# Stores of an output tile as two DMAs, permuted reads on ScalarE, one weight in fp32 on SyncE, and a new order, in a fused attention and token-mixing kernel

## Chip, cores and metric

One core of a Trainium2 chip. The metric is the device time of one execution in microseconds. A profile is one execution, taken by the hardware profiler; its span runs from the first to the last instruction.

## The reference

Attention within chunks of 64 tokens (8 batches, 8 heads, 576 tokens, 64 channels a head), then a mixing block on the joined heads (512 channels):

```python
attn = softmax(q_c @ k_c^T / sqrt(64))        # per chunk of 64
x = (attn @ v_c)  -> (B, S, H * D)            # B=8, S=576, H*D=512
theta = x @ w_theta
zr, zi = x * cos(theta), x * sin(theta)
y = w_tok_r @ zr + w_tok_i @ zi               # over the 576 tokens
u = x + y
out = u + maximum(u @ w_ch, 0)                # float32
```

## The kernel before

The batches are taken in four pairs (0 to 3). The tokens of a pair are 9 tiles of 128 rows: four of each batch, and a middle tile (j = 4, group M) with the last 64 tokens of both. For the attention they form five groups: A and B (first batch), C and D (second), of two tiles each, and M of one.

Every step is written out by hand: ORDER (lines 18 to 60) is a list of names such as `T.0A.1`, a kind, a pair, a group or tile, and sometimes a PSUM slot. The loop at lines 530 to 533 issues them in that order, each engine takes its own instructions in that order, and an in-order engine that waits holds up all behind it. The kinds:

- `q`, `k`, `v` (lines 145 to 182): loads on POOL's DMA queue, which convert fp32 to fp16. q and k of a group share a buffer of the pool `nat` (line 111), which has eight; v has a slot for each tile of two pairs.
- `lt`, `lc`, `lw` (lines 184 to 192): loads of the weights, on POOL too; `lw.00` and `lw.01` are w_tok_r and w_tok_i, 576 KB and 72 KB each in fp16.
- `TW`, `twd`, `twa` (lines 196 to 226): transposes of the token weights on PE, and their copies out of PSUM on DVE and ACT.
- `T`, `tq`, `tk` (lines 230 to 264): transposes of q and k of a group on PE; q is copied by DVE, k by ACT (M's k by DVE). The loads put tokens 2p and 2p+1 on partition p, so the halves come out of the transpose apart; ACT's copy of k puts them together again by writing with a step of two.
- `S`, `e` (lines 266 to 301): scores on PE, exponential on ACT, which writes with a step of two as well.
- `V0`, `V1`, `v0`, `v1` (lines 303 to 336): attention times v for four heads each on PE; DVE divides by the sum of the row (reciprocal at line 328).
- `X`, `x`, `H`, `g`, `z` (lines 338 to 413): transpose of x, its copy on ACT, theta on PE, cosine and sine on ACT, products zr and zi on DVE. For the middle tile two halves change partitions by DMAs on SyncE (lines 410, 411, from `zmid`).
- `Y`, `y`, `U`, `u`, `W`, `w` (lines 417 to 492): for each of the 36 tiles the mixing over tokens on PE (nine accumulating matmuls), plus x on DVE, a transpose, its copy (ACT for even tiles, DVE for odd), the last matmul, relu and sum on DVE into `o` (one of four buffers of `outp`, line 114), and the store to HBM, one DMA on SyncE (line 492). `Y.00` needs zr and zi of groups A, B and M and the whole of wT, thus all three `TW`.

PSUM has three slots of two banks (wide) and two of one bank (thin); Y, U and W use the thin ones. The store of a tile is a DMA whose DRAM side has three dimensions, r (2), t (64) and d (512), as lines 489 to 491 write it: rows 0 to 63 and 64 to 127 of the tile are tokens 128 apart.

Of the kernel before, what the change touches and what calls it, by code (L numbers as in the profile page):

```python
# [18 lines left out]
q.0A new.10 q.0B v.0B init.00 k.0A q.0C q.0M k.0B new.00 v.0A k.0M T.0A.0 tk.0A lt.00
tq.0A S.0A.1 e.0A v.0M T.0B.2 tk.0B V1.0A.0 lw.00 tq.0B v1.0A V0.0A.1 v0.0A S.0B.2 k.0C  # L20
T.0M.0 lw.01 X.0A.1 tq.0M e.0B tk.0M q.1B S.0M.2 x.0A e.0M V1.0B.0 H.0A.1 V0.0M.2 v0.0M
g.0A v1.0B V1.0M.2 V0.0B.0 v1.0M X.0M.2 x.0M v0.0B X.0B.0 q.0D v.0C q.1M TW.00.1 x.0B
H.0M.2 z.0A twd.00 H.0B.0 g.0M k.0D z.0M g.0B T.0C.2 lc.00 twa.00 tq.0C TW.01.0 z.0B
TW.02.1 v.0D twd.01 tk.0C twa.02 S.0C.2 twd.02 twa.01 Y.00.0 Y.01.1 e.0C V1.0C.0 v.1M
y.00 V0.0C.1 q.1A T.0D.2 y.01 k.1M v0.0C U.01.0 tk.0D v1.0C Y.02.1 u.01 tq.0D U.00.0
u.00 y.02 S.0D.1 X.0C.0 e.0D q.1C U.02.1 q.2M Y.03.0 V0.0D.2 u.02 V1.0D.1 v1.0D v0.0D
q.2A x.0C H.0C.0 X.0D.1 T.1M.2 y.03 k.1A W.01.1 tk.1M k.1B q.3A x.0D w.01 W.00.0 tq.1M
U.03.1 H.0D.1 v.1A k.1C g.0C S.1M.2 w.00 u.03 k.2M W.02.0 z.0C w.02 g.0D T.1A.0 z.0D
tk.1A W.03.1 w.03 e.1M T.1B.1 Y.04.0 q.1D V0.1M.2 tq.1A tk.1B tq.1B S.1A.0 V1.1M.1 e.1A
v.2M v1.1M y.04 v0.1M Y.05.1 U.04.0 v.1B u.04 v.1C X.1M.1 V0.1A.0 V1.1A.2 q.3B v0.1A  # L30
W.04.0 v1.1A x.1M S.1B.1 X.1A.0 x.1A y.05 w.04 H.1M.2 U.05.1 u.05 H.1A.0 g.1M g.1A
Y.07.0 y.07 z.1A e.1B q.2B Y.06.1 T.1C.2 v.2B y.06 V0.1B.0 V1.1B.1 U.06.0 tk.1C v.2A
tq.1C W.05.1 q.3C v1.1B S.1C.2 u.06 e.1C k.1D T.2M.1 v0.1B X.1B.0 tq.2M W.06.0 tk.2M
V1.1C.2 x.1B V0.1C.1 w.05 q.3M U.07.1 k.2B v1.1C v0.1C w.06 v.3M u.07 k.3A v.2D H.1B.0
k.3C X.1C.2 T.1D.1 Y.08.0 z.1M x.1C W.07.1 y.08 tq.1D U.08.0 v.1D q.2D H.1C.2 g.1B w.07
z.1B u.08 W.08.1 S.2M.0 tk.1D S.1D.1 e.1D Y.10.0 e.2M w.08 g.1C y.10 k.2A Y.11.1 V0.1D.1
y.11 V1.1D.0 v1.1D Y.12.0 v0.1D X.1D.0 T.2B.2 y.12 T.2A.1 x.1D v.3A U.11.1 U.10.0 tk.2B
H.1D.0 z.1C tk.2A new.20 u.10 u.11 W.11.1 tq.2B tq.2A w.11 Y.13.0 k.3B k.2D g.1D q.2C
U.12.1 S.2B.2 z.1D y.13 u.12 v.3D V1.2M.1 e.2B v1.2M S.2A.0 Y.16.1 y.16 k.2C T.2C.1
tk.2C V0.2M.2 W.12.0 v0.2M w.12 W.10.1 tq.2C e.2A U.13.0 u.13 T.2D.2 X.2M.0 V1.2B.1  # L40
tq.2D w.10 Y.14.0 tk.2D V0.2B.2 x.2M v1.2B V0.2A.0 V1.2A.1 y.14 Y.15.1 U.14.0 v0.2A y.15
v1.2A H.2M.0 u.14 v0.2B Y.17.1 U.16.0 g.2M y.17 X.2B.1 u.16 X.2A.2 S.2C.0 W.13.1 v.3C
W.16.0 w.13 z.2M x.2A U.17.1 u.17 w.16 x.2B H.2A.2 g.2A H.2B.1 z.2A W.17.1 g.2B v.2C
v.3B w.17 Y.18.0 W.14.1 e.2C z.2B T.3A.2 tk.3A k.3M y.18 S.2D.1 V1.2C.0 Y.21.0 w.14
new.30 v1.2C tq.3A U.18.1 e.2D V0.2C.0 S.3A.2 u.18 V1.2D.1 y.21 U.15.0 v1.2D Y.22.1
T.3M.1 v0.2C u.15 e.3A X.2C.2 V0.2D.0 tq.3M Y.20.0 y.22 v0.2D y.20 W.18.1 tk.3M w.18
V0.3A.0 x.2C V1.3A.2 X.2D.1 U.22.0 v0.3A u.22 x.2D q.3D W.15.1 U.20.0 H.2C.0 w.15 u.20
W.20.1 v1.3A w.20 g.2C U.21.0 u.21 H.2D.1 Y.23.1 g.2D T.3B.2 z.2C S.3M.0 T.3C.1 e.3M
y.23 z.2D U.23.0 tk.3C u.23 W.21.1 k.3D tq.3C tq.3B Y.25.0 tk.3B V1.3M.0 w.21 v1.3M
T.3D.1 y.25 tq.3D S.3B.2 V0.3M.0 W.22.1 W.23.0 e.3B V1.3B.2 v0.3M tk.3D X.3A.0 V0.3B.1  # L50
w.22 Y.24.1 x.3A v1.3B v0.3B X.3M.2 S.3D.0 w.23 x.3M X.3B.1 y.24 U.25.0 H.3M.2 e.3D
U.24.1 u.24 u.25 Y.26.0 H.3A.0 y.26 U.26.1 g.3M u.26 Y.27.0 x.3B g.3A W.24.1 z.3M w.24
y.27 H.3B.2 U.27.1 W.25.0 g.3B S.3C.1 z.3A V1.3D.0 u.27 w.25 e.3C Y.28.1 W.27.0 V1.3C.2
z.3B v1.3D y.28 V0.3C.0 V0.3D.1 w.27 v0.3D W.26.1 v0.3C Y.30.0 v1.3C X.3D.1 X.3C.0 w.26
x.3C y.30 Y.31.1 U.30.0 x.3D y.31 u.30 H.3C.2 U.28.1 u.28 U.31.0 H.3D.0 u.31 g.3C W.28.1
W.31.0 g.3D w.28 W.30.1 w.31 z.3C w.30 Y.33.0 z.3D Y.32.1 y.33 y.32 Y.34.0 U.32.1 y.34
U.33.0 u.32 W.32.1 u.33 Y.35.0 w.32 U.34.1 y.35 U.35.0 u.34 W.33.1 u.35 W.34.0 w.33
Y.36.1 w.34 W.35.0 y.36 w.35 Y.37.1 y.37 U.36.0 U.37.1 u.36 u.37 W.36.0 Y.38.1 w.36
W.37.0 y.38 w.37 U.38.1 u.38 W.38.0 w.38
# [500 lines left out]
```

## Time and profile before

| | us |
|---|---|
| runs, median of 3 (lowest to highest) | 301.07 (300.09 to 301.48) |
| profiled execution | 300.1 |
| its span | 298.3 |
| PE matmul busy | 197.9 (66%) |
| ACT busy | 133.1 (45%) |
| DVE busy | 126.4 (42%) |
| POOL busy | 77.5 (26%) |
| granted TensorE clock, mean | 0.876 |

Busy times are of one execution. Matmuls are pipelined and their ends are modelled, so the step from one group's start to that of the next says more of PE's pace than the length of a matmul. SP is SyncE; its instructions are DMA issues and count as no busy time. A wait is put down to what came last.

### The profile page before, as it was taken

Reading aid. Unit: us, or ns where it says so; the run is one execution under the profiler, and the core shown is the slowest. Engines: PE = TensorE matmul, PEld = TensorE weight load, DVE = VectorE, ACT = ScalarE, POOL = GpSimd, SP = SyncE. Lnnn points to the kernel's source line nnn. Section 1 sums busy time; section 2 is a strip of 40 time slices with the busy share of each in tenths; the row PEclk is TensorE's granted clock in tenths of the full one; section 3 lists DMA queues with packets and bytes.
Section 4 is the critical chain, followed back from the end, with each engine's and each line's share of the span. In section 5 each row is a group of like instructions: output and inputs, shape, how many; then the busy total and the mean of one; then the engine's idle time right before and its main releaser. Section 6 shows DMA issues by size and latency. Waiting matters only on the chain.

```text
span 298.3 us, 8370 instructions
## 1 busy us (share of the span) xinstructions
PE 197.9 (66%) x3834; PEld 102.9 (34%) x3834; DVE 126.4 (42%) x248; ACT 133.1 (45%) x137; POOL 77.5 (26%) x100
## 2 busy tenths in 40 slices
PE   0347859698975006969049999998999968762000
PEld 0233425244442002445025545555545424330000
DVE  0044616276476000556016687768486444240000
ACT  1255672387785100858132787586883701000000
POOL 8965759518030017632260000000000000000000
PEclk9999768999999555999758999999999979997555
DMA  9999999999945349996898121111121111111111
GB/s 87 169 193 193 181 170 164 166 82 123 125 63 79 64 71 77 168 159 80 86 67 94 53 63 56 54 53 55 53 66 55 51 51 51 53 51 52 51 51 40
DMA packets 86859, 27.03 MB, mean 91 GB/s; under 512 B 79528, under 2 KB 82216, under 8 KB 86824
## 3 DMA queue, kind: packets, MB, share of 16 engines
q0 software_dynamic: 81504, 16.54, 64.2%
q1 hardware_dynamic: 5320, 9.96, 9.4%
...
q14 instruction: 5, 0.04, 0.0%
...
## 4 chain that ended last, share of the span: by engine, by line
DMA 44%; PE 28%; ACT 9%; POOL 4%; issue 4%; DVE 3%; DVEq 0%; ACTq 0%; POOLq 0%
DMA qk<-in_k_dram 27%; DMA out_dram<-o 17%; PE ps_y L435 10%; PE ps_theta L374 7%; PE ps_uw L471 4%; POOL v L179 2%; ACT kT L259 2%; ACT eT L296 2%; ACT cos L390 2%; POOL qk L158 2%; ACT sin L394 2%; PE ps_uT L453 1%; PE ps_qkT L241 1%; PE ps_x L316 1%; DVE x L329 1%
## 5 line engine op out<-in xcount | busy, mean ns | idle before, releaser
L435 PE MATMUL ps_y<-zr,wT 128*128 128x512 f16 (+1 forms) x180 | 45.2, 404 | 3.9 <-DVE o L480 2.8
L435 PE MATMUL ps_y<-zi,wT 128*128 128x512 f16 (+1 forms) x180 | 46.9, 395 | 0.0
L435 PEld LDWEIGHTS <-wT 128*128 128x128 f16 (+1 forms) x360 | 32.1, 104 | 42.8 <-issue 11.2
L444 DVE TENSOR_TENSOR u<-ps_y,x 128x512 f16<-128x512 f32 x36 | 24.8, 688 | 52.1 <-PE ps_y L435 51.9
L241 PE MATMUL ps_qkT<-id,qk 64*64 64x64 f16 x1152 | 16.2, 207 | 44.8 <-DMA qk<-in_k_dram 27.9
L471 PE MATMUL ps_uw<-wch,uT 128*128 128x512 f16 x144 | 38.5, 400 | 5.9 <-DVE o L480 5.6
L465 ACT COPY uT<-ps_uT 128x512 f16<-128x512 f16 x20 | 11.8, 588 | 65.8 <-PE ps_uT L453 65.8
L480 DVE SCALAR_TENSOR_TENSOR o<-ps_uw,u 128x512 f32<-128x512 f32 x36 | 24.8, 688 | 32.7 <-DMA out_dram<-o 20.2
L374 PE MATMUL ps_theta<-wtheta,xT 128*128 128x512 f16 x144 | 37.2, 405 | 0.2 <-ACT xT L361 0.2
L259 ACT COPY kT<-ps_qkT 128x1024 f16<-128x1024 f16 x16 | 20.8, 1302 | 32.6 <-PE ps_qkT L241 27.8
L179 POOL DMA_DIRECT2D v<-in_v_dram x32 | 28.3, 894 | 27.0 <-DMA qk<-in_q_dram 9.2
L241 PEld LDWEIGHTS <-qk 64*64 64x64 f16 x1152 | 13.5, 118 | 49.4 <-DMA qk<-in_k_dram 28.4
L361 ACT COPY xT<-ps_xT 128x1024 f16<-128x1024 f16 (+1 forms) x20 | 18.3, 927 | 19.3 <-PE ps_xT L349 19.3
L329 DVE TENSOR_TENSOR x<-ps_x,recip 128x512 f16<-128x512 f32 (+1 forms) x40 | 25.5, 638 | 1.4
L390 ACT ACTIVATE cos<-ps_theta,pihalf 128x1024 f16<-128x1024 f32 (+1 forms) x20 | 20.6, 1030 | 9.0 <-PE ps_theta L374 8.9
L296 ACT ACTIVATE eT<-ps_sT 128x1024 f16<-128x1024 f32 x16 | 21.0, 1310 | 6.6 <-PE ps_sT L283 6.5
L257 DVE COPY qT<-ps_qkT 128x1024 f16<-128x1024 f16 (+1 forms) x20 | 12.6, 633 | 22.0 <-ACT kT L259 19.0
L471 PEld LDWEIGHTS <-uT 128*128 128x128 f16 x144 | 13.5, 101 | 21.5 <-issue 8.2
L374 PEld LDWEIGHTS <-xT 128*128 128x128 f16 x144 | 13.9, 103 | 16.0 <-issue 3.6
L328 DVE RECIPROCAL recip<-ps_x 128x8 f32<-128x8 f32 (+1 forms) x40 | 7.8, 195 | 26.0 <-PE ps_x L316 26.0
L394 ACT ACTIVATE sin<-ps_theta 128x1024 f16<-128x1024 f32 (+1 forms) x20 | 18.7, 934 | 0.0
L158 POOL DMA_DIRECT2D qk<-in_q_dram x16 | 14.5, 908 | 13.6 <-PE ps_qkT L241 8.1
...
## 6 DMA issues: line engine op xcount, KB each, us to landing
out_dram<-o SPq DMA_DIRECT2D x36, 256.0 KB
qk<-in_q_dram POOLq DMA_DIRECT2D x16, 256.0 KB, 7.0
...
qk<-in_k_dram POOLq DMA_DIRECT2D x16, 256.0 KB, 9.4
...
qk<-in_q_dram POOLq DMA_DIRECT2D x8, 64.0 KB, 6.8
qk<-in_k_dram POOLq DMA_DIRECT2D x8, 64.0 KB, 6.9
```

The costliest lines, as they stand in the source:

```text
L179: nc.gpsimd.dma_start(v16[:, slot + r, :, 0:D], v[2 * p + bb, :, t0 : t0 + P, :].rearrange("h s d -> s h d"),)
L241: nc.tensor.transpose(psv[half[h], r, e, w, s, :], t[half[r], w, 2 * e + h, s, :], id16[half[r], half[r]],)
L259: nc.scalar.copy(out=t.rearrange("p x c t -> p x (c t)").rearrange("p x (i s) -> p x s i", s=2), in_=ps,)
L296: nc.scalar.activation(out=eT.rearrange("p h r e (i s) -> p (h r e) s i", s=2), in_=ps.rearrange("p (x s i) -> p x s i", s=2, i=CH // 2), ...
L329: nc.vector.tensor_tensor(out=st[p]["x"][:, j0 : j0 + n, f * NE * D : (f + 1) * NE * D].rearrange("p c (h d) -> p c h d", h=NE), in0=psv[: ...
L374: nc.tensor.matmul(ps[:, j * DM : j * DM + DM], xT[:, j * NDB + db, :], wtheta16[:, db, :], start=(db == 0), stop=(db == NDB - 1),)
L390: nc.scalar.activation(out=cos[:, 0:n].rearrange("p a e -> p (a e)"), in_=pin, func=AF.Sin, bias=pihalf, scale=1.0,)
L394: nc.scalar.activation(out=sin[:, 0:n].rearrange("p a e -> p (a e)"), in_=pin, func=AF.Sin)
L435: nc.tensor.matmul(ps[rows], wT[:, kt, cols], z[:, jz, :], start=(i == 0), stop=(i == 2 * KT),)
L444: nc.vector.tensor_tensor(out=u, in0=st[p].pop(("ps_y", j)), in1=st[p]["x"][:, j], op=ALU.add)
L471: nc.tensor.matmul(ps, uT[:, db * P : db * P + P], wch16[:, db, :], start=(db == 0), stop=(db == NDB - 1),)
L480: nc.vector.scalar_tensor_tensor(out=o, in0=st[p].pop(("ps_uw", j)), scalar=0.0, in1=u, op0=ALU.max, op1=ALU.add)
```

## The change

Four things. The store of a tile is two DMAs, one for each half of 64 rows. The exponential and the copy of k write in order and read PSUM with the step instead. The first token weight is loaded as fp32 by SyncE into `wraw` (which takes a buffer of the tag `zi16`) and `wend`, and a new step `cw` casts it to fp16 on ACT. And ORDER is new throughout: it begins with the token weight and group M, puts `TW.00` first on PE, all of pair 0's loads but `v.0D` ahead of `lw.01`, and moves steps everywhere; of the steps only `cw.00` is new. Its beginning:

```
lw.00 q.0M init.00 cw.00 q.0B q.0A TW.00.0 v.0M k.0M q.0C k.0A new.00 T.0M.1 new.10
tq.0M k.0B tk.0M v.0A twd.00 S.0M.2 k.0C T.0A.1 twa.00 lt.00 e.0M V0.0M.0 q.0D T.0B.2
v.0B tq.0A tk.0A S.0A.1 tk.0B tq.0B V1.0M.2 v0.0M v.0C e.0A S.0B.0 V1.0A.1 v1.0M k.0D
v1.0A T.0C.2 V0.0A.1 e.0B tq.0C lw.01 tk.0C X.0M.0 q.1A S.0C.2 v0.0A q.1B x.0M X.0A.0
e.0C q.1M v.0D x.0A H.0M.1 H.0A.2 V1.0B.0 g.0M k.1A v1.0B g.0A V0.0B.1 v0.0B V0.0C.0
v0.0C k.1B V1.0C.1 k.1M v1.0C X.0B.2 T.0D.0 x.0B z.0A q.1C tq.0D tk.0D X.0C.1 x.0C z.0M
H.0B.2 q.2M S.0D.0 lc.00 g.0B v.1M TW.01.1 v.1A twd.01 q.1D TW.02.2 twa.01 twa.02 e.0D
H.0C.1 g.0C q.2B z.0B twd.02 Y.00.0 y.00 Y.02.1 U.00.0 V1.0D.2 T.1A.0 v1.0D u.00 tq.1A
```

The part around the loads of pair 2 and the end:

```
x.1C w.04 e.2M tk.2B u.07 H.1C.2 tq.2B W.07.0 z.1D W.05.1 w.07 q.3D Y.11.0 v.2M w.05
U.10.1 new.20 V1.2M.0 g.1C u.10 S.2A.1 V0.2M.2 y.11 W.08.0 v.3C Y.12.1 e.2A z.1C k.2D
...
U.36.1 u.36 U.34.0 u.34 W.36.1 W.34.0 w.36 w.34 Y.35.1 y.35 U.37.0 U.35.1 u.37 u.35
W.37.0 Y.38.1 w.37 W.35.0 y.38 U.38.1 u.38 W.38.1 w.35 w.38
```

The code:

```diff
+    wraw = pairp.tile([P, KT, S], FP32, name="wraw", tag="zi16")
+    wend = glob.tile([CH, S], FP32, name="wend")
...
     def load_tok(ri):
         ap = (moe_w_tok_r, moe_w_tok_i)[ri]
-        nc.gpsimd.dma_start(
-            wnat[:, 0:KT, ri, :], ap[0 : KT * P, :].rearrange("(a p) s -> p a s", p=P)
-        )
-        nc.gpsimd.dma_start(wnat[0:CH, KT, ri, :], ap[KT * P : S, :])
+        if ri == 0:
+            eng, most, end = nc.sync, wraw, wend
+        else:
+            eng, most, end = nc.gpsimd, wnat[:, 0:KT, 1], wnat[0:CH, KT, 1]
+        eng.dma_start(most, ap[0 : KT * P, :].rearrange("(a p) s -> p a s", p=P))
+        eng.dma_start(end, ap[KT * P : S, :])
+
+    def cast_tok():
+        nc.scalar.copy(out=wnat[:, 0:KT, 0], in_=wraw)
+        nc.scalar.copy(out=wnat[0:CH, KT, 0], in_=wend)
...
             nc.scalar.copy(
-                out=t.rearrange("p x c t -> p x (c t)").rearrange(
-                    "p x (i s) -> p x s i", s=2
-                ),
-                in_=ps,
+                out=t.rearrange("p x c t -> p x (c t)"),
+                in_=ps.rearrange("p x s i -> p x i s"),
             )
...
         nc.scalar.activation(
-            out=eT.rearrange("p h r e (i s) -> p (h r e) s i", s=2),
-            in_=ps.rearrange("p (x s i) -> p x s i", s=2, i=CH // 2),
+            out=eT.rearrange("p h r e c -> p (h r e) c"),
+            in_=ps.rearrange("p (x s i) -> p x i s", s=2, i=CH // 2),
...
         if j == MID:
-            to = out[2 * p : 2 * p + 2, KT * P : S, :]
+            to = [out[2 * p + b, KT * P : S, :] for b in range(2)]
         else:
             bb = int(j > MID)
             jl = j - bb * (MID + 1)
-            s0 = (jl // 2) * GT
-            to = out[2 * p + bb, s0 : s0 + GT, :].rearrange(
-                "(r c t) d -> c r t d", r=2, t=CH
-            )[jl % 2]
-        nc.sync.dma_start(to, o)
+            s0 = (jl // 2) * GT + (jl % 2) * CH
+            to = [out[2 * p + bb, s0 + r * P : s0 + r * P + CH, :] for r in range(2)]
+        for r in range(2):
+            nc.sync.dma_start(to[r], o[half[r]])
```

## Rows read from the trace of the kernel before

**Rows 1.** Page, totals: busy us (share of the span), count, by engine.

```profile
PE 197.9 (66%) x3834; PEld 102.9 (34%) x3834; DVE 126.4 (42%) x248; ACT 133.1 (45%) x137; POOL 77.5 (26%) x100
```

**Rows 2.** Windows by stage: stretch, length, busy by engine, PE clock, DMA share, GB/s.

```profile
0.00:60.00 60.00, 34.67 (x958) 19.37 (x962) 20.33 (x47) 26.37 (x27) 44.55 (x61) 0.91 1.76 165
60.00:155.00 95.00, 57.33 (x1285) 30.25 (x1272) 37.85 (x75) 47.09 (x47) 31.25 (x38) 0.84 0.92 96
155.00:240.00 85.00, 82.36 (x1498) 43.24 (x1496) 55.73 (x108) 57.27 (x60) 1.74 (x2) 0.97 0.25 60
240.00:277.50 37.50, 23.51 (x119) 10.05 (x118) 12.48 (x20) 2.35 (x4) 0.00 (x0) 0.88 0.13 52
277.50:298.30 20.80, 0.00 (x0) 0.00 (x0) 0.00 (x0) 0.00 (x0) 0.00 (x0) 0.50 0.12 47
```

**Rows 3.** Timeline of DVE, last stage: start, us, instruction, idle before and its releaser.

```profile
271.64 0.69 DVE L480 SCALAR_TENSOR_TENSOR o<-ps_uw,u 128x512 f32<-128x512 f32 x1 [3.83 <-DMA out_dram<-o]
276.77 0.69 DVE L480 SCALAR_TENSOR_TENSOR o<-ps_uw,u 128x512 f32<-128x512 f32 x1 [4.44 <-DMA out_dram<-o]
```

**Rows 4.** Chain that ended last, in order of time: start, us, what.

```profile
72.29 42.13 DMA qk<-in_k_dram
...
242.83 33.82 DMA out_dram<-o x2
```

**Rows 5.** Page, DMA issues; timeline of SyncE's queue at the first stores.

```profile
out_dram<-o SPq DMA_DIRECT2D x36, 256.0 KB
...
62.77 18.06 SPq L492 DMA_DIRECT2D out_dram<-o  x5
```

**Rows 6.** Timeline of POOL, and one row of PE, before the second stage's hole ends.

```profile
100.84 0.68 POOL L172 DMA_DIRECT2D v<-in_v_dram  x1 [6.10 <-DMA v<-in_v_dram]
107.56 0.88 POOL L158 DMA_DIRECT2D qk<-in_k_dram  x1 [6.04 <-DMA v<-in_v_dram]
...
114.46 0.64 PE L241 MATMUL ps_qkT<-id,qk 64*64 64x64 f16 x32 [20.81 <-DMA qk<-in_k_dram]
```

**Rows 7.** Timeline of SyncE's queue at 171 us; window just behind it.

```profile
171.07 0.52 SPq L410 DMA_DIRECT2D zr<-zmid  x1
...
173.00:174.00 1.00, 1.00 (x7) 0.46 (x5) 0.51 (x2) 1.00 (x2) 0.00 (x0) 1.00 0.60 97
```

**Rows 8.** Timeline of PE in the dense stretch.

```profile
190.19 0.39 PE L453 MATMUL ps_uT<-id,u 128*128 128x128 f16 x4
190.42 1.89 PE L374 MATMUL ps_theta<-wtheta,xT 128*128 128x512 f16 x8
192.15 1.03 PE L471 MATMUL ps_uw<-wch,uT 128*128 128x512 f16 x4
...
196.99 0.71 PE L241 MATMUL ps_qkT<-id,qk 64*64 64x64 f16 x64
197.52 0.32 PE L283 MATMUL ps_sT<-qT,kT 64*64 64x64 f16 x16
```

**Rows 9.** Timeline of PE at the first y tile.

```profile
41.60 2.31 PE L435 MATMUL ps_y<-zr,wT 128*128 128x512 f16 x5 [1.14 <-DVE wT L223]
```

**Rows 10.** Groups of ACT by shape (busy, mean ns), then DVE's timeline at 28 us.

```profile
L296 ACT ACTIVATE eT<-ps_sT 128x1024 f16<-128x1024 f32 x16 | 21.0, 1310 | 6.6 <-PE ps_sT L283 6.5
L259 ACT COPY kT<-ps_qkT 128x1024 f16<-128x1024 f16 x16 | 20.8, 1302 | 32.6 <-PE ps_qkT L241 27.8 <-DVE qT L257 4.8
...
L394 ACT ACTIVATE sin<-ps_theta 128x1024 f16<-128x1024 f32 x16 | 16.3, 1021 | 0.0
...
27.75 0.17 DVE L328 RECIPROCAL recip<-ps_x 128x4 f32<-128x4 f32 x1
...
28.30 0.20 DVE L328 RECIPROCAL recip<-ps_x 128x8 f32<-128x8 f32 x1
```

**Rows 11.** Page, DMA issues: KB each, median us from issue to landing.

```profile
v<-in_v_dram POOLq DMA_DIRECT2D x8, 64.0 KB, 8.1
```

**Rows 12.** Timeline of PE in the last stage.

```profile
248.17 0.38 PE L453 MATMUL ps_uT<-id,u 128*128 128x128 f16 x4 [0.46 <-DVE u L444]
```

More of the change, by code (lines that the diff above doesn't have):

```diff
@@ L18 @@
 ORDER = """
[L19 to L59, printed above, removed]
+lw.00 q.0M init.00 cw.00 q.0B q.0A TW.00.0 v.0M k.0M q.0C k.0A new.00 T.0M.1 new.10
+tq.0M k.0B tk.0M v.0A twd.00 S.0M.2 k.0C T.0A.1 twa.00 lt.00 e.0M V0.0M.0 q.0D T.0B.2
@@ new lines @@
+V0.0D.1 tk.1A Y.01.0 v.1B v0.0D X.0D.2 T.1M.0 x.0D k.1D k.2B y.02 T.1B.1 y.01 tq.1M
+U.02.1 U.01.0 k.1C k.2M z.0C tk.1B v.1D H.0D.2 u.02 tk.1M u.01 S.1A.0 W.01.1 w.01 g.0D
+e.1A tq.1B W.02.0 Y.03.1 S.1B.2 V0.1A.1 S.1M.0 w.02 z.0D v0.1A e.1B q.2A e.1M Y.04.0
+V1.1M.1 V0.1M.2 y.03 q.3A V1.1A.0 y.04 Y.06.1 v1.1A v1.1M v0.1M T.1D.0 y.06 tq.1D
+V0.1B.1 v0.1B X.1A.2 tk.1D W.00.0 U.03.1 u.03 x.1A X.1M.0 x.1M q.2D T.1C.1 k.2A tk.1C
+w.00 S.1D.2 T.2M.0 U.06.1 u.06 tq.1C W.03.0 H.1M.1 e.1D tk.2M g.1M q.2C tq.2M v.1C
@@ new lines @@
+V1.1B.0 V1.1D.2 w.03 v1.1D Y.05.1 W.06.0 V0.1D.2 v1.1B X.1B.0 x.1B y.05 H.1A.1 z.1M
+v0.1D H.1B.0 Y.07.1 w.06 U.05.0 g.1A X.1D.2 S.1C.1 g.1B y.07 T.2A.0 U.04.1 u.05 z.1B
+q.3B q.3C x.1D v.2B Y.08.0 v.2A H.1D.2 e.1C u.04 V0.1C.1 z.1A tk.2A tq.2A y.08 k.2C
+V1.1C.0 U.08.1 g.1D Y.10.0 v1.1C v0.1C q.3M u.08 S.2M.0 T.2B.1 X.1C.2 y.10 W.04.0 U.07.1
+x.1C w.04 e.2M tk.2B u.07 H.1C.2 tq.2B W.07.0 z.1D W.05.1 w.07 q.3D Y.11.0 v.2M w.05
+U.10.1 new.20 V1.2M.0 g.1C u.10 S.2A.1 V0.2M.2 y.11 W.08.0 v.3C Y.12.1 e.2A z.1C k.2D
@@ new lines @@
+v0.2M w.08 v1.2M T.2C.2 S.2B.1 e.2B V1.2A.0 v1.2A v.2D Y.15.0 v.2C tk.2C V0.2A.0 tq.2C
+y.12 y.15 T.2D.1 v.3A tq.2D v0.2A V1.2B.2 v1.2B Y.14.1 V0.2B.0 tk.2D X.2M.1 y.14 X.2A.2
+U.15.0 x.2M Y.16.1 S.2D.1 x.2A v0.2B X.2B.0 k.3B y.16 S.2C.2 e.2C U.11.1 u.15 W.10.0
+u.11 Y.18.1 w.10 x.2B e.2D y.18 H.2M.2 W.11.0 w.11 U.12.1 H.2A.0 g.2M z.2M V0.2D.1
+V1.2C.2 U.18.0 u.12 W.15.1 u.18 w.15 W.12.0 v.3M w.12 v1.2C g.2A k.3C Y.17.1 V1.2D.0
+k.3A v0.2D y.17 v1.2D T.3A.2 V0.2C.1 k.3M U.16.0 W.18.1 w.18 H.2B.0 u.16 tk.3A v0.2C
@@ new lines @@
+Y.13.0 g.2B U.17.1 tq.3A X.2C.1 y.13 u.17 v.3D T.3M.2 X.2D.0 x.2C U.14.0 W.16.1 u.14
+tq.3M x.2D z.2A U.13.0 u.13 w.16 tk.3M H.2C.1 H.2D.0 g.2C W.13.0 W.14.1 T.3B.2 S.3M.1
+g.2D z.2B w.13 S.3A.0 w.14 tq.3B tk.3B e.3M Y.20.0 Y.21.1 new.30 z.2C k.3D y.20 W.17.0
+e.3A z.2D T.3D.2 V1.3A.1 w.17 tq.3D tk.3D v1.3A v.3B V1.3M.0 Y.24.0 T.3C.2 S.3B.1 v1.3M
+tk.3C y.21 V0.3A.0 y.24 U.20.1 u.20 tq.3C Y.23.0 v0.3A X.3A.2 e.3B V0.3M.0 y.23 S.3C.1
+U.21.1 e.3C W.20.0 u.21 Y.22.1 w.20 v0.3M x.3A y.22 U.24.0 H.3A.1 U.23.1 u.24 u.23
@@ new lines @@
+W.21.0 g.3A Y.28.1 V0.3C.2 V1.3B.0 w.21 v0.3C V0.3B.1 y.28 Y.27.0 W.23.1 v0.3B V1.3C.2
+v1.3B y.27 S.3D.1 w.23 X.3M.0 x.3M e.3D v1.3C Y.25.0 y.25 U.27.1 u.27 H.3M.0 W.24.0 w.24
+V1.3D.2 g.3M V0.3D.1 v1.3D W.27.1 v0.3D Y.26.0 w.27 z.3M U.22.1 y.26 X.3C.2 u.22 X.3D.0
+X.3B.1 W.22.1 w.22 U.28.0 x.3B x.3D u.28 H.3B.1 U.25.1 z.3A u.25 W.28.0 W.25.1 g.3B
+H.3D.0 x.3C w.28 U.26.0 z.3B u.26 w.25 H.3C.1 W.26.1 g.3D g.3C w.26 Y.32.0 Y.30.1 z.3C
+y.32 Y.31.0 y.30 Y.33.1 y.31 z.3D y.33 U.30.0 u.30 U.31.1 U.33.0 u.31 u.33 U.32.1 u.32
@@ L60 @@
+W.30.0 w.30 W.31.1 w.31 W.32.0 Y.37.1 w.32 y.37 Y.36.0 W.33.1 y.36 Y.34.0 w.33 y.34
+U.36.1 u.36 U.34.0 u.34 W.36.1 W.34.0 w.36 w.34 Y.35.1 y.35 U.37.0 U.35.1 u.37 u.35
+W.37.0 Y.38.1 w.37 W.35.0 y.38 U.38.1 u.38 W.38.1 w.35 w.38
 """.split()
@@ L140, in pair @@
         for name in ("x", "zr", "zi"):
-            st[p][name] = pairp.tile([P, NT, DM], FP16, name=name + "16")
+            st[p][name] = pairp.tile([P, NT, DM], FP16, name=name + "16", tag=name + "16")
     def load_qk(p, g, which):
@@ L502 @@
         "lw": lambda p, i: load_tok(i),
+        "cw": lambda p, i: cast_tok(),
         "init": lambda p, g: setup(),
```

## The prediction

> **What bounds the kernel now.** I read the totals first, then busy time by stage, then the chain and the waits inside each stage. The totals [rows 1] name no engine: PE, the busiest, is busy for 197.9 us of 298.3. The stages [rows 2] tell more. From 155 to 240 us PE is busy 82.36 of 85 us; this stretch is bound by PE. Before it, from 60 to 155, PE works 57.33 of 95 us, and after it, from 240 to 277.5, only 23.51 of 37.5. In the last 20.8 us no engine computes at all, yet the DMA column stays at 0.12 to 0.13 and 47 to 52 GB/s. That share is the key: 2 of 16 DMA engines working without pause is 0.125.
>
> The end first. The output tile's operation on DVE waits for an output buffer, and its starts stand 5.13 us apart (271.64, 276.77), each released by a store [rows 3]; five such starts in a row keep this step. 256 KB in 5.13 us is 51 GB/s, the rate of the column. So a store runs on two engines, which fits line 489: its outermost dimension, r, has two entries. The chain agrees: its last long piece is 33.82 us of stores [rows 4]. Four buffers times 5.13 us are the 20.5 us that follow the last compute. All 36 stores [rows 5] take 36 x 5.13 = 184.7 us of a queue that first gets work at 62.77.
>
> Then the middle. One k load issued at 72.29 lands 42.13 us later [rows 4], and PE, whose next transposes need it, stands still for 20.81 us [rows 6]. On POOL the following loads wait for earlier ones for about 6 us each [rows 6], again close to the cadence of a store. My reading: every load needs a part on the two engines where stores are queued, and gets one turn for each store. Both the tail and the hole in the middle are thus the same fault.
>
> **The change, part by part.** *Stores.* Each store becomes two DMAs of 64 rows by 2 KB with the 64 rows outermost. Does such a form spread? The trace has one near relative: the zmid copies on the same SyncE queue, also 64 rows outermost. Where only stores run the share is 0.13 [rows 2]; after two zmid issues at 171 us it reaches 0.60 [rows 7], which is 7.5 engines above the stores' two. So yes, for more than two; I take all 16, which makes a store 5.13 x 2/16 = 0.64 us. SyncE pays a second issue, 0.52 us [rows 7]: 36 x 0.52 = 19 us on a queue with hundreds to spare; behind them stand only the zmid copies, one or two issues late, about 1 us. The output buffers then come free long before they are asked for; the 20.5 us tail and the 5 us steps go, and so does the cause of the 6 us loads. What is late next is PE.
>
> The Trainium skill, "DMA: Bandwidth & Descriptors", section "Rules for kernel authors", speaks against this part: do not split a transfer into its two partition halves, since both halves spray over all 16 engines and serialize. By it the split would gain nothing. The row of 0.13 does not show its premise, since the unsplit store here is not on all 16.
>
> *PE's work.* It does not change: 648 matmuls 512 wide (144 theta, 360 y, 144 w), 3042 of 64 and 144 of 128 (u transposes). In the dense stretch, 8 wide ones take 1.73 us from start to the next group's start, 64 small ones 0.53, four u transposes 0.23 [rows 8]. So 648 x 0.216 + 3042 x 0.0083 + 144 x 0.0575 = 140.0 + 25.2 + 8.3 = 173.5 us at the full clock. The dense stretch had PE busy 0.97 of the time at a granted clock of 0.97 [rows 2]; if both losses counted fully its pace would be 0.94, if they overlap 0.97. I take 0.955.
>
> *Head.* In before, Y.00 starts at 41.60 [rows 9], behind the last wT copy. In the new order more stands in front of it: all of group C's attention and its theta, and the S of D. Counted through ORDER, PE has done 12.8 us of its 173.5 by then. Loads up to lw.01 are 5.8 MB as the DMA counts them (written bytes; the fp32 weight counts 1.33), at 165 GB/s [rows 2] 35 us; before it was 4.3 MB, 26 us, and compute was the later of the two. TW.01, TW.02, their copies and H.0C follow, some 6 us. So Y.00 again at about 42; between 39 and 48, because the fp32 load shares the engines with the first q and k loads.
>
> *First token weight.* POOL loses two issues of some 0.9 and 0.5 us and ACT gains two casts: 2304 and 576 elements wide, at 1.0 ns each (sin: 1021 ns for 1024 [rows 10]) 2.3 + 0.6 = 2.9 us. ACT has nothing else until k.0M has landed; on ACT only twa.00 and e.0M are queued behind, on PE T.0M is queued behind TW.00. A late landing therefore costs the head directly; it is in the 39 to 48. wraw takes a zi16 buffer that pair 1 wants only much later.
>
> *Permuted reads.* 32 ACT operations take 1310 and 1302 ns where sin of the same size takes 1021 [rows 10]. If a stride on the reading side is free, each saves 0.29 us, 9 us of ACT; if it costs as much as on the writing side, nothing. The only strided PSUM read in the trace is DVE's reciprocal: 4 elements 0.17, 8 elements 0.20 us [rows 10], so at most 0.03/4 = 7.5 ns an element, or 7.7 us for 1024. That is the far end. I take 1.1 us, near sin, since that row has the same engine, source and size and the reciprocal is another engine's operation; with ACT at 57 of 85 us in the dense stretch [rows 2], the gain hides behind PE. I count nothing for it.
>
> The Trainium skill, "SBUF — State Buffer", section "Door 1: The DMA port swizzle", says that PSUM is organized in 8-byte lines and that non-contiguous access to it slows matmuls significantly. Whether ACT's reads suffer too no row here shows; were it so, the sum would move towards the ACT rival below.
>
> *Order and buffers.* With the loads fast, what gates them is the eight qk buffers: the n-th group's load waits for the transpose of the group eight before. I followed that for every load of both orders and counted the PE work between release and use. In the new order nearly all have over 13 us. One is short: v.2M stands on POOL behind q.3D, which waits for T.2B, and V1.2M comes 7.0 us of PE work later, 7.3 at this pace. POOL needs 0.9 for q.3D and 1.4 for two v issues [rows 6], and a 64 KB v load 8.1 us to land [rows 11]: 10.4. So PE waits about 3 us; 0 to 5. In before T.2C had a similar slack, 7.9.
>
> **The sum.** Y.00 at 42; then (173.5 - 12.8)/0.955 = 168.3, which gives 210.3; v.2M 3, 213.3. At the end only y, u, w of the last tiles are left, on two PSUM slots, and gaps of 0.46 us for u appear [rows 12]: eight tiles, 4 us, 217.3. After the last Y, y and u lie open, some 1.5; then relu_add 0.69, two issues 1.0, landing 2.5 (between 0.64 of transfer plus about 1, which before's end needs beyond its cadence, and 8.1): 5.7, so 223.0. Before's profiled run took 300.1 us for a span of 298.3, 1.8 outside; so 224.8, and I say 225. Its 300.1 stands 1.0 below the median of the runs, 301.07.
>
> **The rivals.** (a) *The loads stay late.* If the 6 us turns come from something other than the stores, only the end is cured: 298.3 less 20.5, plus 3 for a new landing, less 12 of the steps between 240 and 277.5 (37.5 less 23.51 of PE work [rows 2], with 2 left over), plus 1.8, about 271. For it: the rows name only loads as what POOL waits for [rows 6]. Against it: the turns are as long as a store and a load, and before the first store the rate is 165 GB/s [rows 2]. (b) *The split does not spread.* Two halves of 2.56 us on the same two engines: cadence 5.13, time as before, 300. This is what the Trainium skill's rule on halves, above, would give. If each half ran on one engine, a tile would take 10.3 us and the end would come at 62.8 + 36 x 10.3, about 430. Against both: the 0.60 [rows 7]. (c) *ACT becomes the bound, slower.* Place: e and k copies, with PE waiting for each. ACT has 133.1 - 41.8 + 2.9 = 94.2 us of other work. With some 27 us at the two ends in which ACT cannot work, it overtakes PE's end when 94.2 + 32t exceeds about 197, so from t = 3.2 us; it is slower than before from t = 5.6, and at 7.7 it gives 94.2 + 246 + 27 = 367. For it: the reciprocal's step. Against it: that step is read from two short operations of another engine. (d) *The new order meets waits that I haven't seen*, or PE's clock falls in them: half a microsecond more for each of the 36 tiles is 18 us, 243; 240 to 250.
>
> **How the numbers follow.** Forecast 225: 0.78, its own range 207 to 240: low end Y.00 at 39, pace 0.97, no other waits, 4 at the end, 1.8 outside, 210.5, and 3 less if early work overtakes; high end 48, pace 0.94, 5, 4, 9 at the end, 1.8, 239. Waits (d), 0.04; better than 207, 0.03; (a) 0.06; (c) between 245 and 299, 0.03, above, 0.02; (b) unchanged 0.03, one engine 0.01. The range 207 to 245 takes in the first and most of (d). About 0.5% is what a measurement of this kernel can tell from no change. Faster 0.78 + 0.04 + 0.03 + 0.06 + 0.03 = 0.94, same 0.03, slower 0.03.
>
> **What would show it.** Right: the o operation no longer waits for stores; the DMA share in the last stage is in bursts instead of a level 0.13; the span ends within 5 us of the last DVE operation; k loads land within 10 us throughout; PE over 0.9 busy from about 45 us to near the end. Permuted reads: e and k copies near 1.1 us. Wrong: a level DMA share, waits of POOL of 5 us and more, ACT busier than PE, or Y.00 well after 48.

## The result, and the profile after

The changed kernel takes 237.34 us (median; 235.57 to 239.05) against 300.58 for the one before: ratio 0.79, 95% interval 0.783 to 0.797. It is faster; the forecast was 225, its range 207 to 245. The profiled execution took 235.57 us for a span of 233.8.

The totals and the stages of the changed kernel (busy us by engine; the stages have stretch, length, PE, PEld, DVE, ACT, POOL, PE clock, DMA share, GB/s):

```profile
PE 189.8 (81%) x3834; PEld 101.5 (43%) x3834; DVE 125.9 (54%) x248; ACT 124.2 (53%) x137; POOL 76.3 (33%) x98
...
0.00:60.00 60.00, 31.76 (x988) 19.21 (x989) 19.81 (x46) 30.83 (x32) 44.45 (x60) 0.97 1.80 181
60.00:155.00 95.00, 86.95 (x1972) 47.08 (x1972) 60.11 (x120) 61.65 (x68) 31.80 (x38) 0.98 1.06 117
155.00:200.00 45.00, 44.80 (x727) 23.17 (x726) 30.91 (x61) 28.79 (x32) 0.00 (x0) 1.00 0.32 71
200.00:233.80 33.80, 26.26 (x150) 12.05 (x148) 15.08 (x25) 2.93 (x5) 0.00 (x0) 0.95 0.34 74
```

Against [rows 2] two stages are another kernel's: from 60 to 155 us PE works 86.95 us instead of 57.33, and the 20.8 us at the end in which no engine computed are gone but for 4.2. The first 60 us are not better: 31.76 us of PE against 34.67. ACT has 9 us less [rows 1].

The chain that ended last, by engine, and the last operation of DVE (start, us, idle before and its releaser):

```profile
PE 70%; DVE 9%; issue 8%; DMA 6%; ACT 4%; POOL 1%; DVEq 0%; ACTq 0%; POOLq 0%
...
228.91 0.69 DVE L486 SCALAR_TENSOR_TENSOR o<-ps_uw,u 128x512 f32<-128x512 f32 x1 [1.40 <-PE ps_uw L477]
```

The chain is PE's now, where 33.82 us of stores ended it before [rows 4], and the output operation waits for PE instead of a store [rows 3]. The span ends 4.2 us after it, not 20.8. The DMA issues of the page (KB each, median us to landing):

```profile
out_dram<-o SPq DMA_DIRECT2D x72, 128.0 KB, 2.4
...
wraw<-in_moe_w_tok_r_dram SPq DMA_DIRECT2D x1, 1152.0 KB, 6.2
```

A half tile lands in 2.4 us. No engine that computes waits for a store any more; only SyncE does, for the last two of them, at the end of the program (1.7 us).

The head, PE's timeline at the first y tile, and all of its gaps put down to issue of over 1 us:

```profile
52.16 1.24 PE L441 MATMUL ps_y<-zr,wT 128*128 128x512 f16 x5
...
20.42 0.43 PE L249 MATMUL ps_qkT<-id,qk 64*64 64x64 f16 x15 [2.93 <-issue]
27.27 0.75 PE L249 MATMUL ps_qkT<-id,qk 64*64 64x64 f16 x40 [2.80 <-issue]
33.20 0.32 PE L355 MATMUL ps_xT<-id,x 64*64 64x64 f16 x8 [2.31 <-issue]
48.10 1.15 PE L218 MATMUL ps_wT<-id,wnat 64*64 64x64 f16 x105 [1.22 <-issue]
61.33 0.32 PE L355 MATMUL ps_xT<-id,x 64*64 64x64 f16 x17 [1.67 <-issue]
120.42 0.41 PE L249 MATMUL ps_qkT<-id,qk 64*64 64x64 f16 x27 [3.04 <-issue]
```

"Issue" is time in which PE stands idle and waits for nothing that the profile shows. The first y tile starts at 52.16 us, 10.6 later than before [rows 9]. Most of the 12 us between forecast and result were lost here.

### The profile page after: what moved, and what is told of

Its sections match the earlier page's. It is cut to its first block, busy times and chain, and to the rows that moved or that the text cites. A ratio compares the mean times of both kernels' runs of the same rounds, so it can differ in the third digit from the quotient of the medians.

```text
span 233.8 us, 8436 instructions
## 1 busy us (share of the span) xinstructions
PE 189.8 (81%) x3834; PEld 101.5 (43%) x3834; DVE 125.9 (54%) x248; ACT 124.2 (53%) x137; POOL 76.3 (33%) x98
## 4 chain that ended last, share of the span: by engine, by line
PE 70%; DVE 9%; issue 8%; DMA 6%; ACT 4%; POOL 1%; DVEq 0%; ACTq 0%; POOLq 0%
PE ps_y L441 30%; PE ps_theta L380 14%; PE ps_uw L477 11%; PE ps_qkT L249 4%; PE ps_uT L459 4%; DMA qk<-in_q_dram 3%; DMA qk<-in_k_dram 3%; PE ps_sT L289 3%; DVE u L450 2%; ACT kT L267 2%; DVE x L335 2%; PE ps_x L322 2%; PE ps_xT L355 2%; DVE qT L265 1%; DVE o L486 1%
## 5 line engine op out<-in xcount | busy, mean ns | idle before, releaser
L441 PE MATMUL ps_y<-zi,wT 128*128 128x512 f16 (+1 forms) x180 | 45.4, 391 | 0.1
L441 PE MATMUL ps_y<-zr,wT 128*128 128x512 f16 (+1 forms) x180 | 42.3, 391 | 1.7 <-DVE o L486 1.7
L380 PE MATMUL ps_theta<-wtheta,xT 128*128 128x512 f16 x144 | 37.9, 411 | 1.7 <-ACT wT L234 1.2
L477 PE MATMUL ps_uw<-wch,uT 128*128 128x512 f16 x144 | 35.9, 380 | 0.7 <-ACT uT L471 0.7
L267 ACT COPY kT<-ps_qkT 128x1024 f16<-128x1024 f16 x16 | 16.2, 1015 | 25.0 <-DVE qT L265 20.8
L302 ACT ACTIVATE eT<-ps_sT 128x1024 f16<-128x1024 f32 x16 | 16.4, 1026 | 6.5 <-PE ps_sT L289 6.4
L477 PEld LDWEIGHTS <-uT 128*128 128x128 f16 x144 | 12.9, 98 | 14.3 <-ACT uT L471 1.2
## 6 DMA issues: line engine op xcount, KB each, us to landing
wnat<-in_moe_w_tok_i_dram POOLq DMA_DIRECT2D x1, 576.0 KB, 12.3
```

Source lines behind the costliest of these rows:

```text
L267: nc.scalar.copy(out=t.rearrange("p x c t -> p x (c t)"), in_=ps.rearrange("p x s i -> p x i s"),)
L380: nc.tensor.matmul(ps[:, j * DM : j * DM + DM], xT[:, j * NDB + db, :], wtheta16[:, db, :], start=(db == 0), stop=(db == NDB - 1),)
L441: nc.tensor.matmul(ps[rows], wT[:, kt, cols], z[:, jz, :], start=(i == 0), stop=(i == 2 * KT),)
L477: nc.tensor.matmul(ps, uT[:, db * P : db * P + P], wch16[:, db, :], start=(db == 0), stop=(db == NDB - 1),)
```

## The experiments

The theory to test was that the stores' two engines made both the tail and the late loads; the main rival, that the new order made part of the gain. Later runs ask what the other three parts are worth, and what made the head long. Ratios are to the kernel before, timed on the same chip beside each group of runs.

**Stores alone.** The kernel before with the new stores only (the lines that work out `to` change with them and are left out here):

```diff
...
-        nc.sync.dma_start(to, o)
+        for r in range(2):
+            nc.sync.dma_start(to[r], o[half[r]])
```

> The kernel before with nothing but the store of a tile as two DMAs of 64 rows; its order, its ACT writes and its weight load stay. Theory (stores on two engines cause both the tail and the late loads between 60 and 155 us): nearly the whole gain comes, 228 to 245 us, since PE has about 160 us of work left at 41.6 us; POOL has no more waits of 5 to 6 us, and the o operation no longer waits for stores. Rival (the new order brings the middle's gain, the stores only the tail's): 262 to 280 us.

Measured: 236.77 us, ratio 0.789 (0.785 to 0.794). With nothing but the stores the kernel is as fast as the changed one. Its middle stage:

```profile
60.00:155.00 95.00, 85.68 (x1865) 45.62 (x1866) 59.88 (x117) 66.86 (x68) 33.01 (x39) 0.98 1.10 122
```

In the old order, with the old loads, PE works 85.68 of the 95 us: the hole was due to the stores too. The rival falls, and so does rival (a) of the prediction.

**The old store in the changed kernel** (again without the lines for `to`).

```diff
...
-        for r in range(2):
-            nc.sync.dma_start(to[r], o[half[r]])
+        nc.sync.dma_start(to, o)
```

> The changed kernel with the old store, one DMA per tile whose DRAM side begins with a dimension of two. Theory: the level DMA share of 0.13 and the 5.13 us steps come back, 36 x 5.13 = 184.7 us from the first store at about 67 us at the earliest: 252 us at the very least, and 285 to 310 with late loads. Rival (order and loads make the gain): under 250 us.

Measured: 295.67 us, 0.986 (0.980 to 0.991). The whole wait for stores, and two of the last starts on DVE:

```profile
DVE o L486 <- DMA out_dram<-o: 43.1, 15, 4.5
...
267.52 0.69 DVE L486 SCALAR_TENSOR_TENSOR o<-ps_uw,u 128x512 f32<-128x512 f32 x1 [3.88 <-DMA out_dram<-o]
272.64 0.69 DVE L486 SCALAR_TENSOR_TENSOR o<-ps_uw,u 128x512 f32<-128x512 f32 x1 [4.43 <-DMA out_dram<-o]
```

The steps are 5.12 us again. The other three parts together bring 1.4% here (two runs), where the stores end the kernel and can hide what else they do.

**Two DMAs, but a leading dimension of two.** It separates the number of DMAs from their shape:

```diff
-            nc.sync.dma_start(to[r], o[half[r]])
+            nc.sync.dma_start(
+                to[r].rearrange("(t a) d -> a t d", a=2), o[half[r]]
+            )
```

> The changed kernel with two DMAs per tile as it has them, but the DRAM side of each half written with a leading dimension of two (even rows, then odd rows; the rows of a half land in another order). Bytes, descriptors of 2 KB and number of DMAs are as in the changed kernel. Theory (the leading dimension sets how many engines a store gets): two engines again, a tile in 2 x 2.56 = 5.1 us, 285 to 310 us. Rival (two DMAs instead of one is what matters): 233 to 242 us as the changed kernel.

Measured: 299.19 us, 0.994 (0.990 to 0.998). The stage from 200 us, and two of the last starts:

```profile
200.00:260.00 60.00, 48.46 (x422) 21.93 (x420) 27.41 (x50) 18.05 (x22) 0.00 (x0) 0.91 0.14 54
...
270.72 0.69 DVE L486 SCALAR_TENSOR_TENSOR o<-ps_uw,u 128x512 f32<-128x512 f32 x1 [3.17 <-DMA out_dram<-o]
275.83 0.69 DVE L486 SCALAR_TENSOR_TENSOR o<-ps_uw,u 128x512 f32<-128x512 f32 x1 [4.42 <-DMA out_dram<-o]
```

A share of 0.14 and steps of 5.11 us, with 72 DMAs of 128 KB. So the leading dimension of the DRAM side decides, and splitting by itself is worth nothing.

**Permuted writes back.** The changed kernel with the two ACT operations as before:

```diff
-                in_=ps.rearrange("p x s i -> p x i s"),
+                in_=ps,
...
-            out=eT.rearrange("p h r e c -> p (h r e) c"),
+            out=eT.rearrange("p h r e (i s) -> p (h r e) s i", s=2),
```

> The changed kernel, but exp and the copy of k write with the step of two again and read in order. Theory (ACT's time lies behind PE): e and k copy go from 1026 and 1015 ns back to about 1310 and 1302, 9 us more of ACT, and the time stays within 1% of the changed kernel's 237 us. Rival (ACT is on the chain in the head, where it answers PE group by group): 3 to 6 us slower, 240 to 243 us.

Measured: 238.92 us, 0.796 (0.791 to 0.801). The operations of this run, by shape (busy, mean ns), then those of the changed kernel:

```profile
L304 ACT ACTIVATE eT<-ps_sT 128x1024 f16<-128x1024 f32 x16 | 21.0, 1314 | 5.6 <-PE ps_sT L291 5.5
L267 ACT COPY kT<-ps_qkT 128x1024 f16<-128x1024 f16 x16 | 20.9, 1307 | 22.7 <-DVE qT L265 19.0 <-PE ps_qkT L249 3.7
```

```profile
L302 ACT ACTIVATE eT<-ps_sT 128x1024 f16<-128x1024 f32 x16 | 16.4, 1026 | 6.5 <-PE ps_sT L289 6.4
L267 ACT COPY kT<-ps_qkT 128x1024 f16<-128x1024 f16 x16 | 16.2, 1015 | 25.0 <-DVE qT L265 20.8 <-PE ps_qkT L249 4.2
```

The step costs 0.29 us on the writing side and nothing on the reading side. In time it is 0.7% by the medians, with intervals that overlap (to 0.797 there, from 0.791 here). Not settled by this run; the next one settles it in the old order.

**The old order with new stores and permuted reads**, and the changed kernel itself beside it:

> The changed kernel itself, unaltered, beside the next ones on the same chip: 236 to 239 us. It gives the clock by which differences of 1 to 2 us between them can be told.

> The kernel before with the new stores and the permuted reads, thus the order and the weight load of before. With the stores alone it took 236.8. Theory (new order and fp32 weight together bring nothing, the reads 0.5 to 2 us): 234.5 to 236.5, at or below the changed kernel. Rival (the new order is worth something that the reads need): over 238.

Measured: the changed kernel 236.89 us, 0.789 (0.786 to 0.793); the old order with stores and reads 232.56 us, 0.775 (0.771 to 0.778). Against stores alone (0.785 to 0.794) the intervals are apart: here the reads are worth 4.2 us, 1.5% of the time before, more than I had expected. PE's waits for the exponential and the copy of k, all with stores alone, then all with the reads (us in total, times, longest):

```profile
PE ps_x L316 <- ACT eT L296: 1.7, 4, 0.6
PE ps_sT L283 <- ACT kT L259: 0.7, 1, 0.7
PE ps_sT L283 <- ACT eT L296: 0.5, 1, 0.5
```

```profile
PE ps_x L314 <- ACT eT L294: 0.3, 1, 0.3
```

They fall from 2.9 to 0.3 us, which is more than half of the gain; the rest is not traced. And this kernel beats both: the new order and the fp32 weight, taken together, cost 4.3 us. Its first y tile starts at 39.28 us:

```profile
39.28 2.31 PE L433 MATMUL ps_y<-zr,wT 128*128 128x512 f16 x5 [1.06 <-DVE wT L223]
```

**More loads where there were none.** The changed kernel with 48 more loads behind the last one:

```diff
+    def extra():
+        spare = wnat.rearrange("p a r s -> p (a r s)")[:, 0 : 5 * H * 2 * D]
+        spare = spare.rearrange("p (n x) -> p n x", n=5)
+        for i in range(48):
+            nc.gpsimd.dma_start(
+                spare[:, i % 5].rearrange("p (h e) -> p h e", h=H),
+                q[i % 8, :, 0:GT, :].rearrange("h (p s) d -> p h (s d)", s=2),
+            )
```

> The changed kernel with 48 loads of 256 KB more, issued on POOL behind its last load, into a buffer that nobody reads any more (the natural token weights). They fill the DMA queues from about 118 to 190 us, where the changed kernel's PE has no idle gap put down to issue at all. Theory (those gaps, 2.3 to 3 us each in the first 62 us and again at 117, are PE waiting for its instructions, whose DMA stands behind loads): three or more such gaps of 1 us and more appear between 118 and 195 us, each ending as an instruction packet lands, and the time rises by 4 to 15 us. Rival (they come from something of the head, such as waits the profile doesn't show): no such gap, time within 2 us.

Measured, one run: 242.14 us, 5.3 more than the changed kernel. All of PE's rows behind an issue gap between 123 and 200 us:

```profile
125.90 0.23 PE L468 MATMUL ps_uT<-id,u 128*128 128x128 f16 x1 [0.69 <-issue]
147.41 0.21 PE L258 MATMUL ps_qkT<-id,qk 64*64 64x64 f16 x1 [0.34 <-issue]
161.44 0.28 PE L258 MATMUL ps_qkT<-id,qk 64*64 64x64 f16 x11 [0.30 <-issue]
167.63 0.48 PE L298 MATMUL ps_sT<-qT,kT 64*64 64x64 f16 x21 [2.86 <-issue]
174.11 0.61 PE L486 MATMUL ps_uw<-wch,uT 128*128 128x512 f16 x2 [0.59 <-issue]
```

4.8 us of such gaps in a stretch that had none, and about as much time. I had expected three of over 1 us; one is. The waits list no other wait of PE from 123 to 200 us, where the DMA column stands at 1.7 where the changed kernel has 0.3. So loads in flight make such gaps. They are shorter here than in the head, probably because many wide matmuls, which use up few instructions in much time, stand between the small ones of pair 3; no run tests that.

The instruction packets tell the same. The trace has 30 DMA packets of 16,384 bytes on the instruction queue. Their times have another origin than the span, whose first instruction stands at 10.39 on their clock. Six of them, beside PE's six gaps above (changed kernel, us):

```
packet: start + took = end     PE resumes   difference
28.44 + 0.95 =  29.39          20.42        8.97
35.25 + 0.94 =  36.19          27.27        8.92
41.28 + 0.94 =  42.22          33.20        9.02
56.10 + 0.97 =  57.07          48.10        8.97
69.25 + 0.88 =  70.13          61.33        8.80
128.44 + 0.95 = 129.39        120.42        8.97
```

Less the 10.39, PE resumes 1.4 to 1.6 us after each packet's end. The 14 kept traces have 98 gaps of PE put down to issue, the new ones of the run with more loads among them, and every one ends 1.2 to 1.7 us after the end of such a packet.

**Pair 1's loads held back.**

```diff
+    def hold(p, g):
+        nc.gpsimd.tensor_copy(out=gate[:, 0:1], in_=st[p]["x"][:, GROUPS[g][0], 0:1])
...
-... q.1A S.0C.2 v0.0A q.1B x.0M X.0A.0 e.0C q.1M ... k.1A ... v0.0B V0.0C.0
+... S.0C.2 v0.0A x.0M X.0A.0 e.0C ... v0.0B hold.0B q.1A q.1B q.1M k.1A V0.0C.0
```

> The changed kernel, but POOL holds back pair 1's first q and k loads (1A, 1B, 1M and k.1A) until group B's x is there, at about 41 us, by one copy of a column on POOL; in the changed kernel they start at 24.6 us. Theory (instructions wait behind loads): the gap of 2.3 us at 31 us and that of 1.2 at 47 shrink, the first y tile starts 2 to 5 us earlier than at 52.2, and the time falls by 1 to 4 us unless pair 1 now comes late. Rival (the head's length is the chain of small attention steps, whatever the queues hold): first y tile within 1.5 us of 52.2, time the same or longer.

Measured: 242.10 us, 0.807 (0.803 to 0.811): slower than the changed kernel by 2.2%, so the gain that I had expected did not come. The first y tile came at 50.54, 1.6 us earlier than in the changed kernel's profile (the other profiles with this order and the fp32 weight have 51.39 to 52.69); but then:

```profile
66.18 0.58 PE L379 MATMUL ps_theta<-wtheta,xT 128*128 128x512 f16 x1 [3.24 <-issue]
80.11 0.44 PE L354 MATMUL ps_xT<-id,x 64*64 64x64 f16 x31 [1.91 <-issue]
84.94 0.38 PE L288 MATMUL ps_sT<-qT,kT 64*64 64x64 f16 x23 [2.32 <-issue]
```

The gap at 33 us stayed (2.58; the queues are full of pair 0's own loads then). The one at 47 went, and the loads that were pushed back made three more behind 60. A load moved out of the head takes its gaps along: those of over 1 us sum to 19.7 us here and to 14.0 in the changed kernel, and the time is 5.2 us longer.

**The fp32 weight in the old order.** All of the change but the order, though the weight's load moves to the front with it:

```diff
-q.0A new.10 q.0B v.0B init.00 k.0A q.0C q.0M k.0B new.00 v.0A ... V1.0A.0 lw.00 tq.0B
+lw.00 q.0A new.00 q.0B v.0B init.00 cw.00 k.0A q.0C q.0M k.0B new.10 v.0A ... V1.0A.0 tq.0B
```

> The order of before with new stores, permuted reads and now the first token weight as fp32 on SyncE too, its cast on ACT right behind the start: all of the change but the new order. Without the weight it took 232.6, the changed kernel 236.9. Theory (what the rest costs, 4.3 us, lies in the new order, whose head puts more small attention steps ahead of the first y tile): 231.5 to 233.5 us. Rival (the fp32 load takes DMA time from the first q and k loads, and that is the cost): 235.5 to 238.

Measured: 235.65 us, 0.785 (0.781 to 0.789), above 0.775 without the weight: it costs 3.1 us in this order. The rival was right. PE's first two transposes and its first y tile, then the first two transposes without the weight:

```profile
8.53 0.64 PE L249 MATMUL ps_qkT<-id,qk 64*64 64x64 f16 x32 [8.53 <-DMA qk<-in_q_dram]
12.93 0.64 PE L249 MATMUL ps_qkT<-id,qk 64*64 64x64 f16 x32 [3.75 <-DMA qk<-in_k_dram]
...
44.09 2.32 PE L441 MATMUL ps_y<-zr,wT 128*128 128x512 f16 x5 [1.06 <-DVE wT L231]
```

```profile
5.78 0.64 PE L241 MATMUL ps_qkT<-id,qk 64*64 64x64 f16 x32 [5.78 <-DMA qk<-in_q_dram]
10.37 0.64 PE L241 MATMUL ps_qkT<-id,qk 64*64 64x64 f16 x32 [3.95 <-DMA qk<-in_k_dram]
```

The 1.3 MB that SyncE moves first delay the first q by 2.75 us and the first k by 2.56. By the first y tile the delay is 4.8 us, of which 2.5 are one longer issue gap (5.04 us where the run without the weight has 2.49). The end comes 3.1 us later by the medians; how the two make that up is not traced, and the weight's type and its place at the front are not parted.

**The weight on POOL in the new order.**

```diff
-        if ri == 0:
-            eng, most, end = nc.sync, wraw, wend
...
+        nc.gpsimd.dma_start(
+            wnat[:, 0:KT, ri, :], ap[0 : KT * P, :].rearrange("(a p) s -> p a s", p=P)
+        )
+        nc.gpsimd.dma_start(wnat[0:CH, KT, ri, :], ap[KT * P : S, :])
```

> The changed kernel with its new order, but the first token weight on POOL's queue with conversion as before (first in the queue), and no cast on ACT. Theory (the order is what costs): 237 to 241, no better than the changed kernel, a little worse since 0.66 MB and two issues now stand ahead of q and k. Rival (the fp32 load costs 4 us): 232 to 235.

Measured: 237.83 us, 0.791 (0.787 to 0.794), not to be told from the changed kernel. With the weight first on either queue the new order is no faster; it asks for the weight first, so this does not part the weight's cost from the order's. The order alone lies between 0.6% (0.789 against 0.785, both with the fp32 weight; the intervals overlap) and 2.0% (0.791 against 0.775, both on POOL).

**The first k sooner**, in the old order with stores and reads:

```diff
-q.0A new.10 q.0B v.0B init.00 k.0A q.0C q.0M k.0B new.00 v.0A k.0M
+q.0A k.0A new.10 init.00 q.0B k.0B v.0A q.0M new.00 k.0M v.0B q.0C
```

> The order of before with new stores and permuted reads (232.6 us), with POOL's first loads put as q.0A, k.0A, identity, q.0B, k.0B, v.0A, so that k.0A no longer waits behind two q, two v and the identity. There T.0A had its k at 10.4 us. Theory (the first 10 us are issue time ahead of k.0A and pass through to the end in part): T.0A's second half at 8 to 9 us, the first y tile 0.5 to 2 us earlier than at 39.3, the time 230.5 to 232.5. Rival (the loads of the whole head set the pace, whatever comes first): no change within 0.5 us, or worse because v.0B comes later.

Measured: 232.90 us, 0.775 (0.772 to 0.779): no change. PE's timeline:

```profile
7.15 0.64 PE L241 MATMUL ps_qkT<-id,qk 64*64 64x64 f16 x32 [0.79 <-DMA qk<-in_k_dram]
...
20.23 3.40 PE L372 MATMUL ps_theta<-wtheta,xT 128*128 128x512 f16 x8 [2.98 <-DMA wtheta<-in_moe_w_theta_dram]
...
39.42 2.31 PE L433 MATMUL ps_y<-zr,wT 128*128 128x512 f16 x5 [1.06 <-DVE wT L223]
```

k's part began 3.2 us sooner, and PE then waited 2.98 us for w_theta. The next load in line took the gain.

**One store of 128 rows.** For all tiles but the four middle ones:

```diff
-            to = [out[2 * p + bb, s0 + r * P : s0 + r * P + CH, :] for r in range(2)]
+            nc.sync.dma_start(out[2 * p + bb, jl * P : jl * P + P, :], o)
+            return
```

> The changed kernel with one store DMA of 128 rows for each tile but the four middle ones, 128 rows outermost on both sides (the tile's rows go to 128 tokens in a row, so half of them land at other tokens than they should). Theory (spread is everything, the number of DMAs nothing): 236 to 238 us, the same as the changed kernel within 0.5%. Rival (splitting a tile in two halves costs, since they are two issues and share the engines): 1 to 3 us faster, and landing of a tile clearly shorter than the 2.4 us of a half.

Measured: 235.79 us, 0.786 (0.782 to 0.789). The changed kernel had 0.786 to 0.793, so the two are not parted: what counts is that 64 or 128 rows lead, and not how many DMAs a tile has. A tile landed in 2.0 us:

```profile
out_dram<-o SPq DMA_DIRECT2D x32, 256.0 KB, 2.0
```

## Why the prediction was right, and where it was off

**Stores.** Right in mechanism and in both places. The reading of the leading dimension held; the runs of the stores alone and of the halves with a leading two show it from both sides, and the share of about 2/16 went and came back with it. That a load gets one turn for each store was a reading, and no run tests it apart; shown is that the late loads go with the stores' form. Landing was put at 2.5 us; it is 2.4.

**The sum from the first y tile on.** Forecast: 168.3 for the work, 3 for v.2M, 4 for gaps at the end and 1.5 after the last Y, 176.8 to the last W. Measured: from 52.16 to 228.87, 176.7. The parts differ. v.2M was never waited for. The buffer of q.3D came free with T.2A, not T.2B, by the timeline of POOL:

```profile
92.75 0.89 POOL L160 DMA_DIRECT2D qk<-in_q_dram  x1 [7.45 <-PE ps_uT L459]
```

T.2A ends at about 92.4, beside the u transposes that the row names; T.2B starts at 100.23; so counting eight groups back was too simple where the transposes run in another order than the loads. The gaps at the end sum to 2.6 us. Two of them:

```profile
222.60 0.40 PE L459 MATMUL ps_uT<-id,u 128*128 128x128 f16 x4 [0.56 <-DVE u L450]
227.83 1.04 PE L477 MATMUL ps_uw<-wch,uT 128*128 128x512 f16 x4 [0.73 <-ACT uT L471]
```

What was saved there was lost on pace: 160.7/(176.7 - 2.6) = 0.92 instead of 0.955. The issue gaps at 61 and 120 us and one wait of 1.71 for the o operation are in it, 6.4 us together; without them the pace is 160.7/167.7 = 0.96, as taken. So a wait that never came was made up by gaps that I had not counted, and that the two sums agree to 0.1 us is luck.

**The end.** 4.9 us from the last W to the end of the span, 4.2 forecast; 1.8 outside, as forecast. The profiled run is the lowest of its four, and the median stands 1.8 us above it.

**The head is the step that failed:** "So Y.00 again at about 42; between 39 and 48." It was 52.16, 4 us outside its bounds, and 10.2 of the 12.3 us between forecast and result. I took the landing of lw.01 (forecast 35 us, by the issue at 20.7 and its 12.3 us to landing 33) and put 6 us behind it. But TW.01 stands on PE behind the attention steps of all groups, and began only at 46.7; from there to the first y tile it took 5.5 us, near the 6. So PE was the later of the two, not the loads. Those steps are short, answer each other across engines, and hold the most instructions per microsecond. PE lost 9.3 us to issue in them before 48.1 (the first four rows of the list), where before lost 1.98 and 1.96. These two rows of before, then PE's first row in before and in the changed kernel:

```profile
19.84 0.26 PE L283 MATMUL ps_sT<-qT,kT 64*64 64x64 f16 x1 [1.98 <-issue]
39.56 0.51 PE L210 MATMUL ps_wT<-id,wnat 64*64 64x64 f16 x39 [1.96 <-issue]
```

```profile
5.95 0.65 PE L241 MATMUL ps_qkT<-id,qk 64*64 64x64 f16 x32 [5.95 <-DMA qk<-in_q_dram]
```

```profile
9.10 1.26 PE L218 MATMUL ps_wT<-id,wnat 64*64 64x64 f16 x50 [9.10 <-ACT wnat L196]
```

So 5.3 of the 10 us are instructions that came late. Of the rest, some 5, one piece can be read: PE's first matmul waits for the cast of the fp32 weight and starts at 9.10 us, 3.15 later than in before. The prediction foresaw that a late landing would cost the head, and gave it no time of its own. How much of the 3.15 reaches the first y tile no run shows. In the old order the fp32 weight moved the first y tile from 39.28 to 44.09, half of it one longer issue gap; in the new order I could not part weight from order. The rows of issue in before's waits were there to be read; I took them as a part of the pace.

**Permuted reads.** I took 1.1 us for an operation; they take 1.03 and 1.02, so the bound from the reciprocal was far off and rival (c) with it. "I count nothing for it" was wrong in the old order, where they are worth 4.2 us: ACT is idle for long, but PE's next steps wait for just these operations. In the new order it is 2 us by the medians and unsettled.

**Weight and order.** "it is in the 39 to 48" put the cost of the weight at about nothing; it is 3.1 us in the old order. The order was taken as neutral; it is not better, by any pair of these runs.

**The rivals.** (a) and (b) fell with the stores alone; the halves on a leading two are (b) itself, 299 against 300 forecast for it. Nearest to what happened is (d), waits that I had not seen, though they lay in the head and not at the 36 tiles. Of the signs of being wrong two appeared: Y.00 came 4 us after 48, and POOL waited 8.9 and 7.5 us, but for PE's steps; for loads it waited 2.7 at most. The rule that I weighed beside (b), from the Trainium skill, "DMA: Bandwidth & Descriptors", section "Rules for kernel authors", says not to split into halves. The run of one store of 128 rows does not part whole from halves (0.786 and 0.789), and the store of before shows that an unsplit transfer can be the slow one; here the rule would have had its point only if the unsplit store had spread.
